# Reordering the first batch of an attention and gated-FFN kernel: scores ahead of the ninth turn, a shared last copy, one strided sum, three idle matmuls

## The chip, the core and the metric

The kernel runs on one core of a Trainium2 chip. The metric is the device time in microseconds (us) of one execution. The kernel before takes 767.75 us, the median of 3 runs (767.1 to 768.05). The profile of a kernel is taken of one execution, and its span (first to last instruction) is about 1.8 us shorter than the device time.

The engines go by short names: PE is TensorE, which does the matmuls, and PEld its weight loads; ACT is ScalarE, DVE is VectorE, POOL is GpSimd. The granted clock is the share of its full clock that the profile shows PE was given, over the stretch named.

## The reference

Four batches of 12416 rows of 128 numbers go through an attention with 32 inducing points and then through a gated feed-forward network (width 1536) with a gated residual:

```python
def mab(q, kv):                                   # C = 128
    s = scale * (q @ kv.transpose(0, 2, 1))
    s = s - s.max(-1, keepdims=True)
    a = np.exp(s)
    a /= a.sum(-1, keepdims=True) + 1e-09
    return a @ kv
h = mab(I, x)                                     # I: 32 inducing points
x = mab(x, h)                                     # what goes on
# ...
gelu = 0.5 * g * (1.0 + erf(g * inv_sqrt2))       # g = x @ w_gate
ffn_out = gelu * val @ w_out                      # val = x @ w_val
res_gate = 1.0 / (1.0 + np.exp(-(x @ w_res)))
return (x + res_gate * ffn_out).astype(np.float32)
```

## The kernel before

The first attention of a batch must read all of x before any row of the second one can begin. For batches 2 to 4 this is hidden behind the feed-forward work of the batch before. For the first batch nothing can hide it, and it is that stretch, some 32 us at the start, that the change edits.

x comes in 13 tiles: 12 of 8 blocks (128 rows each) and a last one of a single block. For each tile, DVE casts it to fp16 (`convert_hi`), PE turns it (transposes into PSUM, `turn_pe`) and ACT or DVE copies the result back. PE then takes the scores against the inducing points, ACT their exponentials, POOL adds these up (`step_e`, L168 and L171), and PE forms the weighted sums (`step_s`, L186).

```python
def turn_pe(b, k, eng=act):
    # ...
    for j in range(w):
        pe.transpose(tps[:, j, :], hi_t[b, k][:, j, :], identF)
    if eng is act:
        act.activation(xt[:, :w, :], tps[:, :w, :], AC.Copy, bias=0.0, scale=1.0)
    else:
        eng.tensor_copy(xt[:, :w, :], tps[:, :w, :])
```

The denominator of that softmax takes two strided sums on DVE, one over what POOL has added up, one over the exponentials of tile 11, which POOL does not add:

```python
def total(zb):
    # folded(e): a DVE sum of 128x256 to 128x32
    s = folded(e_of.pop("s"))
    yield pe.matmul(zb, ones, s, start=True, stop=False)
    # ... the exponentials of the tile of index 11
    s = folded(e_t["a", n0 // WIDE * WIDE][:, n0 % WIDE * M:(n0 % WIDE + w) * M])
    pe.matmul(zb, ones, e_t["a", nblk // WIDE * WIDE][:, :M], start=False, stop=False)
    yield pe.matmul(zb, ones, s, start=False, stop=True)
```

The order of the first batch, and what follows it:

```python
for n in range(ntile - 1):
    convert_hi(0, n + 1, ve)
    turn_pe(0, n, act if n < 10 and n % 2 == 0 else ve)
    # ... n == 0: the inducing points are turned, idle(2)
    if n == ntile - 2:
        turn_pe(0, n + 1, act)
    if n >= 1:
        step_e(n - 1)
    # ... n == 1: idle(2)
    if n >= 2:
        step_s(n - 2)
weight_cast(0, act)
step_e(ntile - 2)
step_e(ntile - 1)
weight_cast(1, act)
weight_cast(2, act)
step_s(ntile - 3)
zb = bank_g()[:, :M]
parts_of = total(zb)
next(parts_of)
step_s(ntile - 2)
step_s(ntile - 1)
next(parts_of)
idle(6, bank_g(), P)
weight_cast(3, act)
weight_cast(4, po)
turn_first_h(0, zb)          # reciprocal of zb, then ht = the attention's result, turned
exps("b", 0, 0, half, bank_g())   # the second attention's exponentials, from ht
# ... more of these, and the first layer of the feed-forward network from ht
```

After that the main loop obeys plans, strings in which G is a gate (matmuls, then a Gelu on ACT), P, Q and V are a product with its gates (the product u is DVE's), a number is so many output matmuls, and "i" is `idle(3)`: three matmuls of 512 columns on unused data, whose only purpose is to keep PE busy so that its granted clock does not fall. The first plan begins `"!GGGiPG VG 5GQ 5Q GQG6 P7G"`; "!" is `rest_of_first()`, the third part of the first layer.

The softmax here doesn't subtract the row's maximum and nothing guards it: scores larger than these inputs give would overflow.

Of the kernel before, what the change touches and what calls it, by code (L numbers as in the profile page):

```python
# [9 lines left out]
FP32 = mybir.dt.float32  # L10
# [3 lines left out]
AC = mybir.ActivationFunctionType  # L14
AL = mybir.AluOpType
# [3 lines left out]
def kernel(  # L19
# [23 lines left out]
    M = inducing.shape[0]  # L43
    F = moe_w_gate.shape[1]
    P = 128
# [4 lines left out]
    nblk = N // P  # L50
    PRE = 8
    ntile = (nblk + PRE - 1) // PRE
    Q = 4
    scale = 1.0 / math.sqrt(C)
    AX = mybir.AxisListType.X
# [25 lines left out]
    def bank_g():  # L81
        return ps_g.tile([P, TOK], FP32, name="g", tag="g")
# [54 lines left out]
    def turn_pe(b, k, eng=act):  # L137
        _, w = blocks_of(k)
        xt = sized(p_xt, w, P, "xt")
        xt_t[b, k] = xt  # L140
        tps = bank_g().bitcast(FP16).rearrange("p (k c) -> p k c", c=P)
        for j in range(w):
            pe.transpose(tps[:, j, :], hi_t[b, k][:, j, :], identF)
        if eng is act:
            act.activation(xt[:, :w, :], tps[:, :w, :], AC.Copy, bias=0.0, scale=1.0)
        else:
            eng.tensor_copy(xt[:, :w, :], tps[:, :w, :])


    nacc_t, acc_t, hra_t, hgv_t, ht_t, hf_t, hgt_t = {}, {}, {}, {}, {}, {}, {}  # L150
# [61 lines left out]

    def total(zb):

        def folded(e):
            s = p_sm.tile([P, WIDE], FP32, name="z", tag="z", bufs=5)
            ve.reduce_sum(s, e.rearrange("p (j m) -> p m j", m=M), axis=AX)
            return s

        s = folded(e_of.pop("s"))  # L220
        yield pe.matmul(zb, ones, s, start=True, stop=False)
        n0, w = blocks_of(ntile - 2)
        s = folded(e_t["a", n0 // WIDE * WIDE][:, n0 % WIDE * M:(n0 % WIDE + w) * M])
        pe.matmul(zb, ones, e_t["a", nblk // WIDE * WIDE][:, :M], start=False, stop=False)
        yield pe.matmul(zb, ones, s, start=False, stop=True)

    def idle(n, bank=None, w=TOK):

        bank = bank_f() if bank is None else bank
        for i in range(n):  # L230
            pe.matmul(bank[:, :w], warm[:, :P], warm[:, :w], start=True, stop=True)

    def finish_h(b, hs=None):
        if hs is None:
            hs = bank_g()
            pe.matmul(hs[:, 0:P + 1], strips.rearrange("p q m -> p (q m)"), nacc_t.pop(b),
                      start=True, stop=True)
        rz = p_h.tile([P, 1], FP32, name="rz1", tag="rz1")
        if b == 0:
            ve.tensor_copy(rz, hs[:, P:P + 1])  # L240
        else:
            ve.reciprocal(rz, hs[:, P:P + 1])
        hf = p_h.tile([P, P + 1], FP32, name="nacc", tag="nacc", bufs=1)[:, :P]
        ve.tensor_scalar(hf, hs[:, 0:P], rz, None, op0=AL.mult)
        hf_t[b] = hf

        hra = p_h.tile([P, 2, P], FP16, name="hra", tag="hra")
        hra_t[b] = hra
        po.memset(hra[2 * M:, 0, :], 0.0)
        po.memset(hra[:2 * M, 1, :], 0.0)  # L250
        po.tensor_copy(hra[2 * M:, 1, :], hf[2 * M:, :])
        po.tensor_tensor(hra[3 * M:, 1, :], hf[3 * M:, :], hra[3 * M:, 1, :], AL.subtract)

        if b not in hgv_t:
            hgv_t[b] = p_h.tile([P, F], BF16, name="hgv", tag="hgv")

    def turn_first_h(b, zb):

        na = nacc_t[b]
        tp = bank_g()[:, :P]  # L260
        pe.matmul(tp, na[:, 0:P], strips.rearrange("p q m -> p (q m)"), start=True, stop=True)
        idle(6, None, P)
        zi = e_of["zi"] = p_h.tile([P, M], FP32, name="zi", tag="zi", bufs=1)
        ve.reciprocal(zi, zb)
        ht = p_h.tile([P, P], FP16, name="ht", tag="ht")
        ve.tensor_tensor(ht.rearrange("p (q m) -> p q m", m=M),
                         tp.rearrange("p (q m) -> p q m", m=M),
                         zi.unsqueeze(1).to_broadcast([P, Q, M]), AL.mult)
        ht_t[b] = ht
        hgv_t[b] = p_h.tile([P, F], BF16, name="hgv", tag="hgv")  # L270
# [12 lines left out]
    def first_layer_out(b, c, bank):  # L283
        ve.tensor_scalar(hgv_t[b][:, c:c + TOK], bank, parts, None, op0=AL.mult)
# [54 lines left out]
    def ones_b(b, j0, j1):  # L339
        t0 = j0 // WIDE * WIDE  # L340
        z = e_of["z", b, t0][:, j0 - t0:j1 - t0]
        ve.reciprocal(z, z)

    def weights_b(b, k, j0=0, j1=None, eng=po, by_pe=False):

        n0, w = blocks_of(k)
        j1 = w if j1 is None else j1
        n = j1 - j0
        if j0 == 0:
            rt_t[b, k] = sized(p_rt, w, P, "rt")  # L350
        t0 = (n0 + j0) // WIDE * WIDE
        o = n0 + j0 - t0
        z = e_of["z", b, t0]
        ev = e_of["t", b, t0].rearrange("p (j m) -> p j m", m=M)
        a2 = p_sm.tile([P, PRE, Q, M], FP16, name="a2", tag="a2")
        eng.tensor_tensor(  # L356
            a2[:, :n],
            ev[:, o:o + n, :].unsqueeze(2).to_broadcast([P, n, Q, M]),
            z[:, o:o + n].unsqueeze(2).unsqueeze(3).to_broadcast([P, n, Q, M]), AL.mult)
        rt = rt_t[b, k][:, j0:j1, :]  # L360
        if by_pe:
            def turned():
                tps = bank_f().bitcast(FP16).rearrange("p (k c) -> p k c", c=P)
                for j in range(n):
                    pe.transpose(tps[:, j, :], a2[:, j].rearrange("p q m -> p (q m)"), identF)
                ve.tensor_copy(rt, tps[:, :n, :])
            return turned
        else:
            sy.dma_start_transpose(rt, a2[:, :n].rearrange("p j q m -> p (j q m)"))
# [160 lines left out]
    pieces = []  # L530
# [17 lines left out]
    def weight_cast(i, eng):  # L548
        dst, src, w = pieces[i]
        if eng is act:  # L550
            act.activation(dst, staged.pop(i)[:, :w], AC.Copy, bias=0.0, scale=1.0)
        else:
            eng.tensor_copy(dst, staged.pop(i)[:, :w])
# [5 lines left out]
    def step_e(n):  # L559
        n0, w = blocks_of(n)  # L560
        exps("a", 0, n0, n0 + w, bank_v())
        if n < ntile - 2:
            add_up(n0, w)

    def step_s(n):
        n0, w = blocks_of(n)
        accumulate(0, n0, n0 + w, n == 0, n == ntile - 1)
# [2 lines left out]
    hi_t[0, 0] = p_hl.tile([P, PRE, P], FP16, name="hi", tag="hi")  # L570
    ve.tensor_copy(hi_t[0, 0][:, :half], xf_t[0, 0][:, :half])
    act.activation(hi_t[0, 0][:, half:], xf_t[0, 0][:, half:], AC.Copy, bias=0.0, scale=1.0)
    for n in range(ntile - 1):
        convert_hi(0, n + 1, ve)
        turn_pe(0, n, act if n < 10 and n % 2 == 0 else ve)
        if n == 0:
            i1t_ps = bank_g()
            pe.transpose(i1t_ps[:, :M], ind_f, ident[:M, :M])
            ve.tensor_copy(I1T, i1t_ps[:, :M])
            idle(2)  # L580
        if n == ntile - 2:
            turn_pe(0, n + 1, act)
        if n >= 1:
            step_e(n - 1)
        if n == 1:
            idle(2)
        if n >= 2:
            step_s(n - 2)
    weight_cast(0, act)
    step_e(ntile - 2)  # L590
    step_e(ntile - 1)
    weight_cast(1, act)
    weight_cast(2, act)
    step_s(ntile - 3)
    zb = bank_g()[:, :M]
    parts_of = total(zb)
    next(parts_of)
    step_s(ntile - 2)
    step_s(ntile - 1)
    next(parts_of)  # L600
    idle(6, bank_g(), P)
    weight_cast(3, act)
    weight_cast(4, po)
    turn_first_h(0, zb)
    exps("b", 0, 0, half, bank_g())
# [14 lines left out]
            turned()  # L620
    first_layer(0, TOK, layers[:, TOK:])
    first_layer_out(0, TOK, layers[:, TOK:])
    weight_cast(5, po)
    ones_b(0, half, WIDE)
    weights_b(0, 0, half, PRE)
    for i in range(6, len(pieces)):
        weight_cast(i, po)
    later = [(t0, min(t0 + WIDE, nblk)) for t0 in range(WIDE, nblk, WIDE)]

    gel = konst.tile([P, 1], FP32, name="gel")  # L630
# [2 lines left out]
    def rest_of_first():  # L633
        layers = bank_v()
        first_layer(0, 2 * TOK, layers[:, :TOK])
        rs, hs = layers[:, TOK:TOK + P], layers[:, TOK + P:TOK + 2 * P + 1]
        pe.matmul(rs[:64, :], ht_t[0][:, :64], wR, start=True, stop=True)
        pe.matmul(hs[:, :P], strips.rearrange("p q m -> p (q m)"), nacc_t.pop(0)[:, :P],
                  start=True, stop=True)
        zi = e_of.pop("zi")  # L640
        for q in range(Q):
            pe.matmul(hs[q * M:(q + 1) * M, P:P + 1], zi, ident[:, 0:1], start=True, stop=True)
        first_layer_out(0, 2 * TOK, layers[:, :TOK])
        finish_h(0, hs)
        res_layer(0, ve, rs)

    plan_first = [
        "!GGGiPG VG 5GQ 5Q GQG6 P7G",
        "Q6 GQA 10RP 8A1GQR 3P 7Q",
        "G7Q G7P 7GP6 P4R7 P VGG8G *",  # L650
        "P9 P5A8 P2 4P 12PG 12GVG",
# [245 lines left out]
```

## Time and profile before

| | before |
|---|---|
| device time, median of 3 | 767.75 us |
| span of the profiled execution | 765.3 us |
| its mean granted clock of TensorE | 0.997 |
| first Gelu of the main loop (ACT) | 32.46 us |
| end of the 19th Gelu | 42.89 us |

This is the line of busy shares of the profile page (busy us, share of the span, number of instructions):

```profile
PE 743.0 (97%) x9623; PEld 432.5 (57%) x9623; DVE 737.1 (96%) x739; ACT 744.5 (97%) x1496; POOL 469.2 (61%) x463
```

Three engines are full, so only the stretches where one of them must wait can be shortened. The prediction below reads where they are. The next lines are ACT's timeline in the kernel before, at the start of the main loop; the columns are start, length, engine, line, operation, output<-input, and in brackets the idle time ahead and what ended it.

```profile
32.46 6.66 ACT L432 ACTIVATE ge<-g 128x512 f32<-128x512 f32 x13
39.50 1.08 ACT L432 ACTIVATE ge<-g 128x512 f32<-128x512 f32 x2 [0.38 <-PE g L421]
40.83 2.06 ACT L432 ACTIVATE ge<-g 128x512 f32<-128x512 f32 x4 [0.24 <-PE g L421]
```

ACT runs 13 Gelus without a pause, then waits twice for a slow PE, 0.38 and 0.24 us. The 19 Gelus, all that ACT runs ahead of its first tanh, take 42.89 - 32.46 = 10.43 us.

### The profile page before, as it was taken

The page shows a single profiled execution, that of the slowest core. Times are in us where ns is not written, and L with a number is a line of the kernel's source. Part 1 is how long each engine was busy: PE and PEld are TensorE (multiplying, and loading weights), DVE is VectorE, ACT ScalarE, POOL GpSimd, SP SyncE. Part 2 cuts the span into 40 slices and gives each one's busy share as a digit, 9 for nine tenths or more (in the row PEclk, how much of TensorE's full clock was granted, in tenths as well). Part 3 has the DMA queues.
Part 4 walks back from the last instruction along what each step waited for, and adds up shares of the span by engine and source line. Part 5 has one row for each costly group of instructions (what it writes and reads, how often), then busy time and mean ns, then how long its engine had stood idle before and what let it go on. Part 6 is the DMA issues. An engine that isn't in the chain of part 4 may idle for free.

```text
span 765.3 us, 23989 instructions
## 1 busy us (share of the span) xinstructions
PE 743.0 (97%) x9623; PEld 432.5 (57%) x9623; DVE 737.1 (96%) x739; ACT 744.5 (97%) x1496; POOL 469.2 (61%) x463
## 2 busy tenths in 40 slices
PE   9999999999999999999999999999999999999997
PEld 6555565566555555565655555565565555555554
DVE  5799999999999999989999999999999999999997
ACT  5799999999999999999999999999999999999997
POOL 3646998612786989623486789752277664543444
PEclk9999999999999999999999999999999999999999
DMA  9325597500165578601044567730105431101111
GB/s 360 110 57 144 138 240 159 130 30 30 50 123 117 115 178 208 156 32 43 16 105 87 129 167 194 173 108 30 43 29 118 88 85 43 43 29 43 44 43 46
DMA packets 118449, 78.16 MB, mean 102 GB/s; under 512 B 96672, under 2 KB 99392, under 8 KB 118336
## 3 DMA queue, kind: packets, MB, share of 16 engines
q1 hardware_dynamic: 118288, 76.60, 38.4%
q8 instruction: 75, 1.23, 0.6%
q14 instruction: 38, 0.31, 0.1%
q10 hardware_dynamic: 48, 0.02, 0.0%
HBM read 27.87 MB, written 25.43 MB: 70 GB/s over the span
## 4 chain that ended last, share of the span: by engine, by line
PE 47%; ACT 33%; issue 10%; DVE 6%; DMA 1%; POOL 1%; SPq 0%; DVEq 0%; ACTq 0%; POOLq 0%
ACT ge L432 24%; PE f L455 21%; PE g L421 12%; PE v L421 7%; DVE u L426 5%; PE g L463 3%; ACT th L469 3%; ACT at L474 3%; DMA xf<-in_x_dram 1%; ACT fe L483 1%; ACT e L171 1%; PE g L168 1%; DVE th L487 1%; POOL lo L127 1%; ACT L171 1%
## 5 line engine op out<-in xcount | busy, mean ns | idle before, releaser
L426 DVE TENSOR_TENSOR u<-ge,v 128x1024 bf16<-128x1024 f32 x584 | 670.8, 1211 | 5.1 <-PE v L421 1.3
L432 ACT ACTIVATE ge<-g 128x512 f32<-128x512 f32 x1164 | 605.3, 659 | 1.8 <-PE g L421 1.6
L455 PEld LDWEIGHTS <-u 128*128 128x128 bf16 x4656 | 269.8, 98 | 214.3 <-issue 209.7
L455 PE MATMUL f<-wO,u 128*128 128x128 bf16 x4656 | 373.6, 220 | 4.1 <-DVE th L487 0.8
L421 PE MATMUL g<-rt,hgv 32*128 32x512 f16 x1152 | 335.7, 379 | 7.3
L421 PE MATMUL v<-rt,hgv 32*128 32x512 f16 x1152 | 221.5, 385 | 1.8 <-DVE u L426 1.4
L488 POOL TENSOR_TENSOR at<-at,th 128x512 f32<-128x512 f32 (+1 forms) x99 | 123.7, 1250 | 130.0 <-ACT ge L432 37.6
L421 PEld LDWEIGHTS <-hgv 32*128 32x128 bf16 x2400 | 73.7, 91 | 85.8 <-issue 20.0
L484 POOL TENSOR_TENSOR th<-th,fe 128x512 f32<-128x512 f32 (+1 forms) x33 | 39.7, 1202 | 97.1 <-ACT fe L483 97.1
L356 POOL TENSOR_TENSOR a<-e,z 128x1024 f16<-128x1024 f32 (+1 forms) x48 | 89.8, 1881 | 6.8 <-DMA rt<-a 3.6
L127 POOL TENSOR_TENSOR lo<-xf,hi 128x1024 f16<-128x1024 f32 x36 | 76.9, 2137 | 0.2
L463 PE MATMUL g<-hra,rt 128*128 128x128 f16 x768 | 71.4, 219 | 1.5
L474 ACT ACTIVATE at<-g 128x512 f32<-128x512 f32 (+1 forms) x100 | 63.9, 649 | 0.2
L469 ACT ACTIVATE th<-g 128x512 f32<-128x512 f32 (+1 forms) x100 | 63.5, 647 | 0.3 <-PE g L421 0.2
L463 PEld LDWEIGHTS <-rt 128*128 128x128 f16 x768 | 50.6, 97 | 10.2 <-issue 8.0
L487 DVE SCALAR_TENSOR_TENSOR th<-th,f 128x512 f32<-128x512 f32 (+1 forms) x67 | 45.4, 678 | 3.2 <-PE f L455 1.7
L121 POOL CAST hi<-xf 128x1024 f16<-128x1024 f32 x36 | 37.4, 1039 | 14.4 <-DMA xf<-in_x_dram 10.4
L485 POOL TENSOR_TENSOR at<-at,fe 128x512 f32<-128x512 f32 (+1 forms) x33 | 39.7, 1203 | 0.0
L332 POOL TENSOR_TENSOR a<-e 128x512 f32<-128x512 f32 (+1 forms) x12 | 15.5, 1289 | 22.2 <-ACT e L171 22.2
L168 PEld LDWEIGHTS <-xt 128*128 128x128 f16 x768 | 23.3, 96 | 3.1 <-issue 2.5
L171 ACT ACTIVATE e<-g 128x512 f32<-128x512 f32 (+3 forms) x40 | 20.9, 602 | 1.9 <-PE g L168 1.8
L335 POOL TENSOR_TENSOR a<-a 128x256 f32<-128x256 f32 (+8 forms) x48 | 20.0, 417 | 3.8
(138 smaller groups left out, 262.3 us busy)
## 6 DMA issues: line engine op xcount, KB each, us to landing
out_dram<-at SPq DMA_DIRECT2D x96, 256.0 KB, 2.1
xf<-in_x_dram SPq DMA_DIRECT2D x39, 512.0 KB, 4.2
ge<-in_x_dram SPq DMA_DIRECT2D x9, 512.0 KB, 7.0
rt<-a SPq DMA_TRANSPOSE x48, 3.1
xt<-hi SPq DMA_TRANSPOSE x36, 3.6
ge<-in_moe_w_gate_dram SPq DMA_DIRECT2D x1, 512.0 KB, 8.9
ge<-in_moe_w_val_dram SPq DMA_DIRECT2D x1, 512.0 KB, 7.6
ge<-in_moe_w_out_dram SPq DMA_DIRECT2D x1, 512.0 KB, 6.8
```

What stands on the lines that cost most here:

```text
L127: eng.tensor_tensor(lo[:, :w, :P], xf_t.pop((b, k))[:, :w, :], hi_t[b, k][:, :w, :], AL.subtract)
L356: eng.tensor_tensor(a2[:, :n], ev[:, o:o + n, :].unsqueeze(2).to_broadcast([P, n, Q, M]), z[:, o:o + n].unsqueeze(2).unsqueeze(3).to_broad ...
L421: pe.matmul(*t[n], start=True, stop=True)
L426: ve.tensor_tensor(u[:, :n], ge_t.pop(value)[:, :n], v_t.pop(value)[:, :n], AL.mult)
L432: act.activation(ge_t[i][:, h * TOK:h * TOK + n], gb[:, :n], AC.Gelu, bias=0.0, scale=1.0)
L455: pe.matmul(self.ffn[:, k, :], u_t[self.gi, si][:, o:o + P], wO[:, fc, :], start=first, stop=not self.todo, skip_group_check=True)
L463: pe.matmul(bank[:, k * P:(k + 1) * P], rt_t[self.b, self.k][:, self.j0 + k, :], hra_t[self.b][:, s, :], start=True, stop=True)
L469: act.activation(self.th[:, :self.tw], self.mix(0), AC.Tanh, bias=0.0, scale=0.5)
L474: act.activation(self.at[:, :self.tw], self.mix(1), AC.Copy, bias=0.0, scale=1.0)
L484: po.tensor_tensor(th, th, fe, AL.mult)
L487: ve.scalar_tensor_tensor(th, th, 1.0, f, AL.add, AL.mult)
L488: (ve if self.gi == ngrp - 1 else po).tensor_tensor(at, at, th, AL.add)
```

## The change

The change wants the first batch to end sooner and the clock to hold at the start of the main loop. The ninth turn, whose tile arrives late, moves behind scores and sums that are ready. The last tile's cast goes to POOL and the last big copy is split between DVE and ACT. The two strided sums become one addition and one sum. ACT's four weight casts move behind the last exponentials of the first attention, so that these are not held up. DVE's third scaling of the first layer gets ahead of a reciprocal that waits for POOL. Three idle matmuls are added behind the second product ("VGi"), and seven small ones are taken out. Two changes are easy to miss in the diff: without the condition `n < 10` the copy of tile 10 goes from DVE to ACT, and the copy of the small last tile goes from ACT to DVE.

```diff
--- before.py
+++ after.py
@@ -141,10 +141,11 @@
         tps = bank_g().bitcast(FP16).rearrange("p (k c) -> p k c", c=P)
         for j in range(w):
             pe.transpose(tps[:, j, :], hi_t[b, k][:, j, :], identF)
-        if eng is act:
-            act.activation(xt[:, :w, :], tps[:, :w, :], AC.Copy, bias=0.0, scale=1.0)
-        else:
-            eng.tensor_copy(xt[:, :w, :], tps[:, :w, :])
+        h = w // 2 if eng is None else w * (eng is not act)
+        if h > 0:
+            ve.tensor_copy(xt[:, :h, :], tps[:, :h, :])
+        if h < w:
+            act.activation(xt[:, h:w, :], tps[:, h:w, :], AC.Copy, bias=0.0, scale=1.0)
 
 
     nacc_t, acc_t, hra_t, hgv_t, ht_t, hf_t, hgt_t = {}, {}, {}, {}, {}, {}, {}
@@ -212,17 +213,15 @@
 
     def total(zb):
 
-        def folded(e):
-            s = p_sm.tile([P, WIDE], FP32, name="z", tag="z", bufs=5)
-            ve.reduce_sum(s, e.rearrange("p (j m) -> p m j", m=M), axis=AX)
-            return s
-
-        s = folded(e_of.pop("s"))
-        yield pe.matmul(zb, ones, s, start=True, stop=False)
+        s = e_of.pop("s")
         n0, w = blocks_of(ntile - 2)
-        s = folded(e_t["a", n0 // WIDE * WIDE][:, n0 % WIDE * M:(n0 % WIDE + w) * M])
-        pe.matmul(zb, ones, e_t["a", nblk // WIDE * WIDE][:, :M], start=False, stop=False)
-        yield pe.matmul(zb, ones, s, start=False, stop=True)
+        e = e_t["a", n0 // WIDE * WIDE][:, n0 % WIDE * M:(n0 % WIDE + w) * M]
+        ve.tensor_tensor(s[:, :w * M], s[:, :w * M], e, AL.add)
+        z = p_sm.tile([P, WIDE], FP32, name="z", tag="z", bufs=5)[:, :M]
+        ve.reduce_sum(z, s.rearrange("p (j m) -> p m j", m=M), axis=AX)
+        yield
+        pe.matmul(zb, ones, e_t["a", nblk // WIDE * WIDE][:, :M], start=True, stop=False)
+        yield pe.matmul(zb, ones, z, start=False, stop=True)
 
     def idle(n, bank=None, w=TOK):
 
@@ -259,7 +258,7 @@
         na = nacc_t[b]
         tp = bank_g()[:, :P]
         pe.matmul(tp, na[:, 0:P], strips.rearrange("p q m -> p (q m)"), start=True, stop=True)
-        idle(6, None, P)
+        idle(5, None, P)
         zi = e_of["zi"] = p_h.tile([P, M], FP32, name="zi", tag="zi", bufs=1)
         ve.reciprocal(zi, zb)
         ht = p_h.tile([P, P], FP16, name="ht", tag="ht")
@@ -570,36 +569,41 @@
     hi_t[0, 0] = p_hl.tile([P, PRE, P], FP16, name="hi", tag="hi")
     ve.tensor_copy(hi_t[0, 0][:, :half], xf_t[0, 0][:, :half])
     act.activation(hi_t[0, 0][:, half:], xf_t[0, 0][:, half:], AC.Copy, bias=0.0, scale=1.0)
-    for n in range(ntile - 1):
+    for n in range(ntile - 2):
+        if n == 8:
+            step_e(n - 1)
+            step_s(n - 2)
+        if n == 9:
+            step_s(n - 2)
         convert_hi(0, n + 1, ve)
-        turn_pe(0, n, act if n < 10 and n % 2 == 0 else ve)
+        turn_pe(0, n, act if n % 2 == 0 else ve)
         if n == 0:
             i1t_ps = bank_g()
             pe.transpose(i1t_ps[:, :M], ind_f, ident[:M, :M])
             ve.tensor_copy(I1T, i1t_ps[:, :M])
             idle(2)
-        if n == ntile - 2:
-            turn_pe(0, n + 1, act)
-        if n >= 1:
+        if n >= 1 and n != 8:
             step_e(n - 1)
         if n == 1:
             idle(2)
-        if n >= 2:
+        if n >= 2 and n not in (8, 9):
             step_s(n - 2)
-    weight_cast(0, act)
+    convert_hi(0, ntile - 1, po)
+    turn_pe(0, ntile - 2, None)
+    turn_pe(0, ntile - 1, ve)
+    step_e(ntile - 3)
+    step_s(ntile - 4)
+    step_e(ntile - 1)
     step_e(ntile - 2)
-    step_e(ntile - 1)
-    weight_cast(1, act)
-    weight_cast(2, act)
     step_s(ntile - 3)
+    step_s(ntile - 2)
+    for i in (0, 1, 2, 3):
+        weight_cast(i, act)
     zb = bank_g()[:, :M]
-    parts_of = total(zb)
-    next(parts_of)
-    step_s(ntile - 2)
+    denominator = total(zb)
+    next(denominator)
     step_s(ntile - 1)
-    next(parts_of)
-    idle(6, bank_g(), P)
-    weight_cast(3, act)
+    next(denominator)
     weight_cast(4, po)
     turn_first_h(0, zb)
     exps("b", 0, 0, half, bank_g())
@@ -620,11 +624,6 @@
             turned()
     first_layer(0, TOK, layers[:, TOK:])
     first_layer_out(0, TOK, layers[:, TOK:])
-    weight_cast(5, po)
-    ones_b(0, half, WIDE)
-    weights_b(0, 0, half, PRE)
-    for i in range(6, len(pieces)):
-        weight_cast(i, po)
     later = [(t0, min(t0 + WIDE, nblk)) for t0 in range(WIDE, nblk, WIDE)]
 
     gel = konst.tile([P, 1], FP32, name="gel")
@@ -641,11 +640,16 @@
         for q in range(Q):
             pe.matmul(hs[q * M:(q + 1) * M, P:P + 1], zi, ident[:, 0:1], start=True, stop=True)
         first_layer_out(0, 2 * TOK, layers[:, :TOK])
+        weight_cast(5, po)
+        ones_b(0, half, WIDE)
+        weights_b(0, 0, half, PRE)
+        for i in range(6, len(pieces)):
+            weight_cast(i, po)
         finish_h(0, hs)
         res_layer(0, ve, rs)
 
     plan_first = [
-        "!GGGiPG VG 5GQ 5Q GQG6 P7G",
+        "!GGGiPG VGi 5GQ 5Q GQG6 P7G",
         "Q6 GQA 10RP 8A1GQR 3P 7Q",
         "G7Q G7P 7GP6 P4R7 P VGG8G *",
         "P9 P5A8 P2 4P 12PG 12GVG",
```

Lines of the changed kernel are numbered a little differently: the Gelu of L432 is L431, the scores of L168 are L169, the sums of L186 are L187.

## The prediction

> **What bounds the kernel now.** I read the table of busy shares first: PE 97%, DVE 96%, ACT 97% of a span of 765.3 us. Three engines are full, so no single one gives much. Then I cut the span into three stretches by the table of windows: the first batch (to 32.46 us, where ACT starts its first Gelu), the run-in of the main loop (32.46 to 46), and the rest.
>
> ```profile
> core 0: us, PE busy (x) PEld busy (x) DVE busy (x) ACT busy (x) POOL busy (x), PEclk, DMA share, GB/s
> 33.73:37.14 3.41, 2.76 (x23) 0.95 (x22) 3.38 (x4) 3.41 (x8) 3.10 (x7) 1.00 0.19 38
> 37.14:40.57 3.43, 3.21 (x25) 1.54 (x24) 3.43 (x4) 3.01 (x6) 0.62 (x1) 0.51 0.42 81
> ...
> 32.46:46.00 13.54, 12.32 (x112) 5.72 (x111) 12.98 (x16) 12.88 (x27) 5.47 (x9) 0.87 0.16 31
> 46.00:745.00 699.00, 685.66 (x8766) 395.42 (x8762) 688.70 (x665) 697.54 (x1407) 440.86 (x424) 1.00 0.39 97
> ```
>
> The last line says what the change can be worth. From 46 to 745 us ACT is busy 697.54 of 699.00 us: it has 1.46 us of holes. All the edits lie before about 36 us, and the order of ACT's work after that is unchanged. So the end moves by two things only: how much earlier ACT starts its first Gelu (32.46 now), and how much of ACT's idle 0.66 us (13.54 - 12.88) in the run-in goes away. The second line shows where that idle time is from: for 3.43 us PE ran at a granted clock of 0.51.
>
> Next the chain of waits, in order of time, through the first batch:
>
> ```profile
> 4.79 11.07 DMA xf<-in_x_dram
> ...
> 15.88 0.75 DVE hi L121
> ...
> 16.68 0.62 PE g L143 x8
> 17.30 0.34 PE v L168 x8
> 17.64 0.57 PE f L186 x16
> 18.21 0.55 PE g L143 x8
> ...
> 22.22 0.74 POOL a L211
> ...
> 22.98 0.61 DVE z L217
> ...
> 24.85 0.29 DVE nacc L198
> 25.14 0.51 DVE z L217
> ...
> 26.76 0.30 DVE ht L266
> ```
>
> The ninth tile of x (tile 8) lands at 15.86; until then the DMA queues are the bound and no reordering helps. From 16.68 PE is nearly gapless (turns L143, scores L168, sums L186, one set per tile each 1.32 us) to the end of the last sums at 24.8. Then comes the flaw that the change aims at: the second strided sum (L217, the tile of index 11) starts only at 25.14, although its exponentials were ready at 23.13, because on DVE it is queued behind the copy of the accumulator. The reciprocal, and with it ht at 26.76, follow that sum. The first exponentials of the second half follow ht at 27.46. The last look is at the timeline of ACT and DVE around them:
>
> ```profile
> 24.57 1.05 ACT L551 ACTIVATE wV<-ge 128x1024 bf16<-128x1024 f32 x1
> 27.46 0.73 ACT L171 ACTIVATE e<-g 128x128 f32<-128x128 f32 x2 [1.83 <-PE g L168]
> ...
> 32.18 0.65 DVE L284 TENSOR_SCALAR hgv<-v,parts 128x512 bf16<-128x512 f32 x1
> ```
>
> ACT has 1.83 us of slack before the second exponentials.
>
> **What the Trainium skill says.** (1) "TensorE: Matmul & The Clock Gate", Part 1: the clock is either half or full, decided over free-running windows of 3413 ns. The trace agrees: the slow spell is 3.43 us at about 0.5, and the 3.41 us before it is the window that failed. Where the windows fall is a matter of phase, so one run need not repeat another's. (2) The same page, Part 4: transposes do not count as PE activity in the same way. No run shows this yet; it matters if PE now waits between transposes. (3) "PSUM — Partial Sum Buffer", section on bank collisions: two reading engines must be kept apart on one bank too. That bears on the shared copy: its halves read one bank, and the built kernel has ACT's half wait for DVE, so they run one after the other. (4) "VectorE: DVE Perf Modes", the tier table: a reduction has only the plain mode. Here a 128x256 reduction takes 0.60 us.
>
> **The change part by part.** I walk the new queue of each engine with durations of the trace. From instruction start to the next engine's start: a turn 0.65, scores 0.39. PE per turn 0.46, scores 0.28, sums 0.57. ACT: a big copy 1.02, exponentials 0.38. DVE: a cast or copy 0.68. POOL: an add 0.73.
>
> Ninth turn. The scores of tile 7 wait for a DVE copy that is queued behind the cast of tile 8, so it ends at 17.22 in both kernels. Before, PE used the wait for the turn of tile 8 (16.68 to 17.25). Now that turn comes after scores 7 and sums 6, at 18.14. Nothing is saved: PE idles 0.6 us more, ACT's copy of tile 8 starts at 18.79 in place of 17.33, and scores 8 begins at 19.87 in place of 18.6. Turn 10 moves to 20.15, its ACT copy lasts until 21.84, and the exponentials of tile 9 to 22.12 behind it (20.70 before).
>
> Small last tile. Its cast moves from DVE (0.22 us, at 20.80) to POOL, queued behind the add of tile 9: 22.26 + 0.73 = 22.98, then about 0.27 (wR's cast of the same shape took 0.29 there). Its turn stands ahead of scores 10 in PE's queue, so PE, done with turn 11 at about 21.92, waits to about 23.30. This is 1.4 us of new waiting.
>
> Last big copy shared: half on DVE (about 0.36), then half on ACT (0.6). It is ready at about 23.1, before it can be used.
>
> Tail. Scores 10 to 23.64, sums 9 to 24.21, scores 12 and 11 to 24.53, their exponentials to 25.05 (23.13 before). Sums 10, 11, 12 on PE to 25.77. POOL's last add ends at 25.03, DVE's new add (128x256, about 0.38, scaled from 1.21 for 128x1024) at 25.45, the one reduction at 26.02. The denominator's matmul starts at 26.10 (25.70 before), the reciprocal at 26.54 (26.15), ht at 26.93 (26.76: there the six idle matmuls had delayed it). The one reduction in place of two takes back about 0.5 us and the idle ones 0.2, of the nearly 1 us that PE lost. Net: ht 0.17 us later.
>
> Weight casts. All four are now behind the last exponentials: 0.52 + 0.52 + 0.94 + 0.94 = 2.92 us by their spacing in the trace, from 25.0 to 27.9. The second exponentials, ready at 27.6, start at 27.9 (27.46). ACT then has 0.6 us less slack, but the 1024-wide exponentials wait for PE in any case (28.95 before, 29.12 now). So the first Gelu starts about 0.17 us later.
>
> Scaling ahead of the reciprocal. The third scaling of the first layer (32.18) now runs at about 31.6, as it no longer waits for POOL's sums. That is worth 0.56 on DVE, of which 0.44 goes to POOL's later start: the first product u begins at about 33.7 in place of 33.82, a gain of 0.1 us that DVE, not ACT, gets.
>
> Three more idle matmuls behind the second product: 3 x 0.21 = 0.64 us of PE, in the window that failed its test, mostly where PE waited for DVE. If the clock holds, ACT's 0.62 us of waits for PE (0.38 at 39.1, 0.24 at 40.6) mostly go: 0.45 us net.
>
> Sum: +0.17 for the start and -0.45 if the clock holds, say two in three: about -0.15 expected. As my walk may overstate the wait for POOL's cast (the exact queue of that moment decides), I shade it to -0.45: 767.75 - 0.45 = 767.3.
>
> **Rivals.** *The tail gets its full gain.* If the small cast does not hold PE, PE ends its sums near 24.5, and ht comes at about 25.9; ACT's casts then end near 26.8 and the second exponentials start 0.6 to 0.9 us earlier; with the clock held the time is about 766.4. For it: the old tail's 2.0 us between ready exponentials and their sum is real. Against it: POOL's queue order, add 9 and then the cast. *A cold spell moves to the first batch.* New PE gaps of 0.8 and 1.4 us and fewer idle matmuls could make a window at 20 to 27 us fail; at half clock one set of turn, scores and sums takes up to twice its 1.32 us, and as about one such set in a window lies on the path, it costs some 1 us: 768.5 to 769 (an estimate). Against it: the old kernel kept 1.00 there with 0.7 us of gaps. *ACT's casts become the bound*, if the exponentials end still later than 25.05: each 0.1 us later is 0.1 us lost, 768.2.
>
> **Range and chances.** All of it moves within about 1.2 us either way, and the three runs before already span 0.95 us. Predicted 767.3, range 766.3 to 768.5. Two per cent would be 15 us, twenty times any term: within 2% is near certain.
>
> **What would show it.** The copy of tile 8 on ACT near 18.8. A wait of PE for POOL's cast at 22 to 23.3 (if absent, my main loss falls). ACT casts ending within 0.3 us of the second exponentials. First Gelu at 32.6. Granted clock 1.00 from 37 to 41, and no ACT wait for PE at 39 to 41. I am wrong if the first Gelu moves by more than 0.6 us either way, or if ACT gains or loses time after 46 us.

## The result

The changed kernel takes 766.93 us, the median of 4 runs (766.53 to 767.04); before in the same rounds takes 767.78 (767.1 to 768.05, 4 runs). The ratio is 0.9989, with a 95% interval of 0.9972 to 1.0007. Ratios here are the mean time of one kernel's runs over that of the other's of the same rounds, so they are not quite the ratio of the medians. The difference of the medians is -0.85 us, which these four runs alone do not tell from zero.

The stretches of the changed kernel, in the columns of the table of windows in the prediction (stretch, us, busy us of PE, PEld, DVE, ACT, POOL with counts, granted clock, DMA share, GB/s):

```profile
0.00:32.46 32.46, 28.98 (x535) 20.17 (x536) 18.88 (x42) 20.26 (x34) 13.73 (x26) 1.00 0.71 273
32.46:46.00 13.54, 12.50 (x116) 5.75 (x115) 12.59 (x17) 12.88 (x28) 5.55 (x9) 1.00 0.16 31
46.00:745.00 699.00, 685.92 (x8767) 395.63 (x8766) 688.95 (x665) 697.70 (x1407) 440.56 (x424) 1.00 0.39 97
```

The clock is 1.00 in the run-in (0.87 before). Yet ACT is busy for the same 12.88 us of it as before, and from 46 us on nothing changed that could matter (697.70 against 697.54). Both facts need an explanation, and the first batch comes first. Its chain of waits, in order of time (start, length, engine, output, line):

```profile
20.75 1.02 ACT xt L148
...
22.19 0.72 POOL a L212
22.91 0.24 POOL his L121
23.20 0.23 PE g L143
24.52 1.32 PE f L187 x34
...
27.07 0.30 DVE ht L265
```

The walk of the prediction is here step for step: POOL's add of tile 9, then its small cast (`his`), then PE's turn of it at 23.20 (predicted 23.30), the last sums, and ht at 27.07 (26.93; before 26.76). ACT's timeline in the changed kernel:

```profile
18.81 1.02 ACT L148 ACTIVATE xt<-g 128x1024 f16<-128x1024 f16 x1 [0.74 <-PE g L143]
22.68 0.60 ACT L148 ACTIVATE xt<-g 128x512 f16<-128x512 f16 x1 [0.63 <-DVE xt L146]
...
27.77 0.72 ACT L172 ACTIVATE e<-g 128x128 f32<-128x128 f32 x2
32.77 3.51 ACT L431 ACTIVATE ge<-g 128x512 f32<-128x512 f32 x7
36.93 6.03 ACT L431 ACTIVATE ge<-g 128x512 f32<-128x512 f32 x12 [0.65 <-PE g L420]
```

The copy of tile 8 starts at 18.81 (predicted 18.79). The second half of the shared copy waits 0.63 us for DVE's half, so the halves run one after the other. The second exponentials start at 27.77, with no wait behind the weight casts. The first Gelu comes at 32.77, 0.31 us later than before.

The last line holds the surprise. The two waits of before, 0.62 us together, are gone, and one of 0.65 us stands in their place, at 36.28. PE's timeline shows why:

```profile
34.86 0.37 PE L420 MATMUL g<-rt,hgv 32*128 32x512 f16 x1
35.17 0.82 PE L230 MATMUL f<-lo 128*128 128x512 f16 x3
36.14 0.44 PE L454 MATMUL f<-wO,u 128*128 128x128 bf16 x5
```

The new idle matmuls (L230) stand behind a gate and ahead of five output matmuls and the next gate. In before the output matmuls began at 35.10; now they begin at 36.14, and the gate that ACT waits for is behind them.

In these two profiled executions the 19th Gelu ends at 42.89 before and at 42.96 after, and the executions themselves took 767.10 and 767.01: they are equal. So where do the medians' 0.85 us come from? The executions of before that the experiments ran beside their kernels, 20 in all, show it. Here they are by their mean granted clock:

| mean clock | executions of before | mean time, us |
|---|---|---|
| 0.999 | 3 | 766.38 |
| 0.997 | 4 | 767.08 |
| 0.994 and 0.995 | 8 | 767.79 |
| 0.992 | 5 | 768.60 |

In the profiled execution of before (0.997) one window of 3.43 us ran at 0.51, which lowers a mean over 765.3 us by 3.43 x 0.49 / 765.3 = 0.0022. So the rows stand, by this estimate, for none, one, two and three slow windows, and each costs about (768.60 - 766.38) / 3 = 0.74 us. The profile before showed one of the milder executions. The sorting is rough: a mean clock also takes in the end of the run, and one profiled execution with one slow window (e3 below) has 0.998. The four executions of the changed kernel all had 0.999 or 1.000.

### The profile page after: what moved, and what is told of

It is laid out like the page before. It is cut to its first block, busy times and chain, and to the rows that moved or that the text cites. A ratio compares the mean times of both kernels' runs of the same rounds, so it can differ in the third digit from the quotient of the medians.

```text
span 765.2 us, 23976 instructions
## 1 busy us (share of the span) xinstructions
PE 742.3 (97%) x9617; PEld 431.6 (56%) x9617; DVE 736.2 (96%) x738; ACT 745.6 (97%) x1497; POOL 468.7 (61%) x464
## 4 chain that ended last, share of the span: by engine, by line
PE 47%; ACT 34%; issue 9%; DVE 5%; POOL 2%; DMA 1%; SPq 0%; DVEq 0%; ACTq 0%; POOLq 0%
ACT ge L431 25%; PE f L454 21%; PE g L420 12%; PE v L420 7%; DVE u L425 4%; PE g L462 3%; ACT th L468 3%; ACT at L473 3%; DMA xf<-in_x_dram 1%; ACT fe L482 1%; PE g L169 1%; ACT e L172 1%; DVE th L486 1%; POOL lo L127 1%; ACT L172 1%
## 5 line engine op out<-in xcount | busy, mean ns | idle before, releaser
L431 ACT ACTIVATE ge<-g 128x512 f32<-128x512 f32 x1164 | 605.5, 660 | 1.8 <-PE g L420 1.6
L169 PEld LDWEIGHTS <-xt 128*128 128x128 f16 x768 | 23.2, 96 | 4.5 <-issue 2.7
L482 ACT ACTIVATE fe<-f 128x512 f32<-128x512 f32 (+1 forms) x33 | 21.0, 637 | 0.0
```

Of the source, the lines that this page charges most:

```text
L431: act.activation(ge_t[i][:, h * TOK:h * TOK + n], gb[:, :n], AC.Gelu, bias=0.0, scale=1.0)
```

## The experiments

The theory to be tested had three parts. The clock: the three idle matmuls are what makes the changed kernel faster, all else together loses a little. The front: the ninth turn and the small cast on POOL cost the 0.31 us of the first Gelu and hide a gain of the tail. The placement: the idle matmuls behind the gate cost 0.65 us that they need not. The rivals were that the reordering of the first batch gives the gain, that the small cast alone is the cause of the front's loss, and that ACT would wait about as long wherever the idle matmuls stand.

Three groups of kernels ran, each group beside its own runs of before, with medians of 767.49 (9 executions), 767.56 (10, which include those of the first group) and 768.22 (10). All gave correct results. Where kernels of different groups are compared below (the changed kernel with any other, e1 with e11, e8 with e9 and e10), it is by their medians and their traces, and not by a ratio of the same rounds. Every experiment's row also gives the end of the 19th Gelu in its profiled execution, for a reason that the table shows.

| kernel | median us (lowest to highest, executions) | ratio to before, 95% interval | first Gelu | end of 19th | profiled execution |
|---|---|---|---|---|---|
| before | 767.78 (767.1-768.05, 4) | 1 | 32.46 | 42.89 | 767.10 |
| after | 766.93 (766.53-767.04, 4) | 0.9989, 0.9972-1.0007 | 32.77 | 42.96 | 767.01 |
| e1_idle_alone | 766.82 (766.65-767.88, 5) | 0.9997, 0.9983-1.0011 | 32.50 | 42.68 | 766.82 |
| e2_no_idle | 768.15 (767.69-768.58, 5) | 1.001, 0.9998-1.0023 | 32.64 | 44.01 | 768.43 |
| e3_small_cast_dve | 766.65 (766.36-767.69, 5) | 0.9992, 0.998-1.0005 | 32.57 | 43.85 | 767.69 |
| e4_ninth_undone | 766.2 (766.07-767.29, 6) | 0.9987, 0.9975-1.0 | 32.16 | 42.35 | 766.08 |
| e5_both_undone | 765.65 (765.46-766.67, 5) | 0.998, 0.9967-0.9992 | 31.57 | 41.75 | 765.55 |
| e6_idle_ahead | 766.44 (766.28-766.62, 5) | 0.9987, 0.9974-1.0001 | 32.99 | 42.82 | 766.62 |
| e7_whole_copy | 765.93 (765.38-766.31, 4) | 0.9981, 0.9967-0.9994 | 31.40 | 41.58 | 765.38 |
| e8_best | 764.67 (764.46-766.32, 5) | 0.9969, 0.9957-0.9982 | 30.99 | 40.82 | 764.67 |
| e9_two_sums | 765.9 (765.71-766.52, 6) | 0.9977, 0.9964-0.999 | 32.13 | 41.96 | 765.82 |
| e10_scaling_behind | 764.99 (764.61-766.34, 6) | 0.9966, 0.9953-0.9978 | 31.01 | 40.84 | 764.75 |
| e11_before_idle_ahead | 766.38 (766.25-767.25, 6) | 0.9984, 0.9971-0.9997 | 32.53 | 42.36 | 766.42 |

The profiled time less the end of the 19th Gelu is 723.7 to 724.4 us in every row. So what follows differs by 0.7 us at most, where the end of the 19th Gelu differs by 3.2 us (40.82 to 44.01): most of what sets these kernels apart is decided in the first 44 us, and two numbers of a profile are enough to compare them: when the first Gelu starts, and how long the first 19 take.

### e1_idle_alone: the idle matmuls alone, added to before

```diff
-        "!GGGiPG VG 5GQ 5Q GQG6 P7G",
+        "!GGGiPG VGi 5GQ 5Q GQG6 P7G",
```

> The kernel before with nothing but the three idle matmuls behind the second product. Theory A (the measured 0.85 us is the clock: the kernel before falls to half clock near 37 us in most executions, the idle matmuls prevent it): granted clock 1.00 from 30 to 46 us, time 0.6 to 1.2 us under the kernel before, so as fast as or faster than the changed kernel, because the first Gelu stays at 32.46 and is not 0.31 us later. Theory B (the gain is from the first batch's new order or from the scaling of the first layer going ahead): time within 0.3 us of the kernel before, as the idle matmuls only delay the first products by about 0.9 us, as in the trace of the changed kernel (36.14 against 35.10).

Measured: 766.82 us, 0.67 under before's median of this group. The means are nearer (ratio 0.9997, and its interval includes 1). The 19 Gelus took 10.18 us in the profiled execution at a clock of 1.00, with the same wait of ACT, 0.65 us. By the medians this one letter gives nearly as much as the whole change, which is in the range of theory A, that the gain is the clock's. By the ratio of the means it would be theory B's "within 0.3 us". One execution of the five, the slowest (767.88), has a clock of 0.997. So this run leans to theory A and does not settle it; e2, which takes the letter out again, does.

### e2_no_idle: the changed kernel without the added idle matmuls

```diff
-        "!GGGiPG VGi 5GQ 5Q GQG6 P7G",
+        "!GGGiPG VG 5GQ 5Q GQG6 P7G",
```

> The changed kernel without the three idle matmuls. Theory A: the clock falls to a half for one window near 37 us in the trace, ACT waits for PE there, and the time is 0.3 to 0.5 us over the kernel before, the loss of the new order standing alone (first Gelu 0.31 us later). Theory B: about as the changed kernel, 0.5 to 1 us under the kernel before.

Measured: 768.15 us, 0.66 over before of its group; all five executions have a clock of 0.992 to 0.995. First the line of the table of windows of this kernel, then one of ACT's timeline:

```profile
34.93:45.05 10.12, 9.96 (x76) 5.37 (x75) 8.33 (x8) 8.18 (x17) 2.77 (x4) 0.50 0.21 42
```

```profile
40.27 1.08 ACT L431 ACTIVATE ge<-g 128x512 f32<-128x512 f32 x2 [0.53 <-PE g L420]
```

The clock is half for 10.12 us, three windows of 3.4 where I had expected one, and ACT is busy 8.18 us of them. The 19 Gelus take 11.37 us, 1.18 more than the 10.19 in the changed kernel. The four executions of the changed kernel had a clock of 0.999 or 1.000, so in these runs the three idle matmuls are what holds it. Without them the change gains nothing: by the median it is a small loss, which its interval (0.9998 to 1.0023) does not tell from zero. This also shows the spell at its full length, which the profiled execution of before did not.

### e3_small_cast_dve: the last tile's cast back on DVE

```diff
-    convert_hi(0, ntile - 1, po)
+    convert_hi(0, ntile - 1, ve)
```

> The changed kernel with the cast of the small last tile back on VectorE. If PE's wait of 1.0 us for that cast at 22.2 to 23.2 us is what delays the tail (my step): the turn of the small tile follows turn 11 directly, at about 22.0, scores 10 at 22.1, the first Gelu about 0.9 us earlier than in the changed kernel (near 31.9), time 0.7 to 1.0 us under the changed kernel. Rival: scores 10 wait for ACT's copy of tile 10 (to 21.8) and the exponentials behind the shared copy, and the gain at the first Gelu is under 0.4 us.

Measured: 766.65 us, 0.28 under the changed kernel, with the first Gelu at 32.57, 0.20 earlier. The profiled execution happened to be this kernel's slowest; the first batch can still be read from it, as its slow window comes later:

```profile
35.00:38.42 3.42, 3.27 (x21) 1.29 (x21) 1.50 (x2) 1.67 (x5) 2.63 (x4) 0.50 0.19 38
```

So the idle matmuls did not hold the clock here. They start at 34.96, as the slow window begins, run at half clock, and ACT waits 1.75 us for the eighth gate in place of 0.65. They make a slow window rare and do not rule it out: of the 57 executions of the kernels that have them, 7 have a clock of 0.996 or 0.997, besides this one; of before's 20, 17 have 0.997 or less. PE's timeline of the first batch:

```profile
21.96 0.22 PE L143 MATMUL g<-identF,his 128*128 128x128 f16 x1
...
23.36 0.64 PE L187 MATMUL f<-xf,e 128*32 128x128 f32 x13 [0.65 <-issue]
```

The turn of the small tile now runs at 21.96 instead of 23.20, as intended. But PE pauses 0.65 us inside the sums of tile 9, between the third and the fourth matmul, with no releaser in the trace ("issue"), and most of the win is gone. So undoing the cast alone does not win the front back: my expectation fell, and the rival's size, a gain of less than 0.4 us, was right, though not for the rival's reason. The pause sits at a fixed place. In the thirteen profiles, the pauses of PE of over 0.1 us without a releaser between 8 and 33 us come after the same number of its records (matmuls and weight loads): after 450 (0.10 to 0.41 us) or after 706, which is this one (0.65 here, 0.21 in e1). The two are 256 records apart, and the place does not move with the program. What the pause is stays open.

### e4_ninth_undone: the ninth turn in its old place, the cast still on POOL

```diff
-        if n == 8:
-            step_e(n - 1)
-            step_s(n - 2)
-        if n == 9:
-            step_s(n - 2)
         convert_hi(0, n + 1, ve)
# ...
-        if n >= 1 and n != 8:
+        if n >= 1:
             step_e(n - 1)
# ...
-        if n >= 2 and n not in (8, 9):
+        if n >= 2:
             step_s(n - 2)
```

> The changed kernel with only the ninth turn back ahead of the scores and sums; the small cast stays on GpSimd. Theory N (the ninth turn's order is the whole loss in the first batch; GpSimd's cast is then early enough): first Gelu within 0.2 us of the run with both undone (31.57), time near 765.7. Theory C (GpSimd's queue also costs once the rest is fast: add 9, then the cast, then add 10): PE waits for the cast again, for some 0.5 us near 21.4 to 22.5, first Gelu near 32.0 to 32.3, time near 766.3.

Measured: 766.2 us, 0.73 under the changed kernel, the first Gelu at 32.16, 0.61 earlier. PE's timeline:

```profile
22.59 0.23 PE L143 MATMUL g<-identF,his 128*128 128x128 f16 x1 [1.17 <-POOL his L121]
```

PE still waits 1.17 us for POOL's cast, only 0.6 us earlier. So the moved ninth turn costs 0.6 us by itself. Theory C, that POOL's queue costs too once the rest is faster, held: the first Gelu and the time are where it put them, though the wait is 1.17 us and not 0.5. Theory N, that the ninth turn is the whole loss, fell.

### e5_both_undone: both of these undone

```diff
# e4's edit, and
-    convert_hi(0, ntile - 1, po)
+    convert_hi(0, ntile - 1, ve)
```

> The changed kernel with the small cast back on VectorE and the ninth turn back ahead of the scores and sums. If the reordering at the ninth turn only makes PE idle 0.6 us longer (my step): a further 0.4 to 0.6 us earlier than with the cast alone, first Gelu near 31.4, time 1.2 to 1.6 us under the changed kernel. Rival: the ninth turn's order is hidden behind the DMA landings of tiles 9 and 10 or behind ACT's copies, and this run equals the one with the cast alone within 0.2 us.

Measured: 765.65 us, 1.28 under the changed kernel; the first Gelu at 31.57, 1.20 earlier. PE's timeline:

```profile
22.95 0.35 PE L169 MATMUL v<-I1T,xt 128*128 128x32 f16 x8 [0.32 <-ACT e L172]
```

The scores of tile 11 run at 22.95 with only 0.32 us of waiting ahead. The time is in the expected range. In the profiles the two gains do not add: 0.20 and 0.61 alone, 1.20 together. With the ninth turn back, the cast is worth 0.59 (e4 to e5); with the cast back, the ninth turn is worth 1.00 (e3 to e5), of which up to 0.65 is the pause of e3, nearly absent here (the sixteen matmuls take 0.80 us). So the two faults cost about 0.6 us each, and they are what kept the better tail from showing.

### e6_idle_ahead: the changed kernel with its idle matmuls ahead of the gate

```diff
-        "!GGGiPG VGi 5GQ 5Q GQG6 P7G",
+        "!GGGiPG ViG 5GQ 5Q GQG6 P7G",
```

> The changed kernel with its three idle matmuls ahead of the gate matmul of that step in place of behind it. Theory P (behind it they stand in the way of the first products, and ACT's wait of 0.65 us for the eighth gate at 36.3 comes from them; ahead of it PE has time to spare): clock still 1.00 to 46 us, ACT's wait there under 0.2 us, time 0.4 to 0.65 us under the changed kernel, near 766.4. Rival: the eighth gate waits for something else (GpSimd's cast of the output weights, a bank), ACT's wait stays, time as the changed kernel; or the clock falls in some executions and the time spreads to 767.5.

Measured: 766.44 us, 0.49 under the changed kernel. PE's timeline:

```profile
34.92 0.82 PE L230 MATMUL f<-lo 128*128 128x512 f16 x3
35.67 0.38 PE L420 MATMUL g<-rt,hgv 32*128 32x512 f16 x1
35.99 0.45 PE L454 MATMUL f<-wO,u 128*128 128x128 bf16 x5
```

The same three matmuls run at nearly the same time. But now it is the seventh gate that stands behind them (35.67), which ACT reaches only at 36.0, and the eighth runs at 36.37 instead of 36.51 although the first Gelu is 0.22 us later. PE's pauses ahead of the seventh gate (0.09 us) and ahead of the output matmuls (0.15, from 35.99 to 36.14) in the changed kernel are gone. ACT's wait of 0.65 us is gone too; its single records show pauses of 0.09 and 0.10 us in its place. The 19 Gelus take 9.83 us (10.19 behind the gate), at a clock of at least 0.998 in all executions. Theory P, that the place makes the wait, held: the clock does not need that place. Of the 0.65 us, 0.36 came back in the profile.

### e7_whole_copy: e5 with the last big copy whole on DVE

```diff
-    turn_pe(0, ntile - 2, None)
+    turn_pe(0, ntile - 2, ve)
```

> The run with both undone, with the last big copy whole on VectorE, not shared. Theory S (sharing is a loss: ACT's half waits for VectorE's half as both read one PSUM bank, and the exponentials of tile 10 queue behind it): exponentials of tile 10 about 0.5 us earlier (near 22.0), scores of tile 11 near 22.5, first Gelu 0.2 to 0.45 us earlier than 31.57, time near 765.3. Rival: the tail is set by PE's sums, and the first Gelu does not move by over 0.1 us.

Measured: 765.93 us (765.38 to 766.31) against e5's 765.65 (765.46 to 766.67). The two overlap, so the time does not settle it. In the profiled executions e7 is the earlier one, 31.40 against 31.57. These 0.17 us are less than theory S asked for (0.2 to 0.45), more than the rival's 0.1, and within what the front varies by itself (see e8), so neither is shown. No gain of sharing the copy is seen: its halves read one bank one after the other (ACT waits 0.48 us for DVE's half in e5), and ACT's part lies ahead of ACT's exponentials of tile 10, which start at 22.52 in e5 and at 21.83 here.

### e8_best: e7 with the idle matmuls ahead of the gate

```diff
-        "!GGGiPG VGi 5GQ 5Q GQG6 P7G",
+        "!GGGiPG ViG 5GQ 5Q GQG6 P7G",
```

> Both undone, whole copy on VectorE, and the idle matmuls ahead of the gate matmul. If the gains add: 0.4 to 0.65 us under the run with the whole copy, 764.7 to 765.0, some 2.6 us under the kernel before. Rival: the earlier ramp is bound by VectorE's chain ahead of the first product u, or the clock falls, and the time is not under 765.3.

Measured: 764.67 us, 2.9 under before and 2.3 under the changed kernel, and faster than before beyond doubt (interval 0.9957 to 0.9982). Its run-in, in the table of windows:

```profile
30.99:46.00 15.01, 14.13 (x134) 6.67 (x132) 14.40 (x18) 14.81 (x31) 7.39 (x10) 1.00 0.16 35
```

The first Gelu is at 30.99 and ACT is then busy for 14.81 of 15.01 us. The 19 Gelus take 9.83 us, as in e6: the gains of front and placement add in the profile. The time is 1.26 us under e7's, more than the 0.4 to 0.65 expected; the placement gives 0.35 of that (10.18 to 9.83). The front is 0.41 us earlier than e7's although its program is the same, through a shorter pause of PE in the sums of tile 9 (0.81 us for the sixteen matmuls, 1.10 in e7) and about 0.1 us of an earlier landing of tile 8. So single profiles of the front differ by 0.2 to 0.4 us for no reason of the program. One execution of e8 took 766.32 at a clock of 1.000; its cause is open.

### e9_two_sums: e8 with before's denominator

```diff
# total() as in before: two strided sums, the first of which has its matmul
# ahead of the sums of the last, small tile
```

> The best kernel so far (764.67) with the old denominator: two strided sums on VectorE, the second behind the copy of the accumulator, in place of an add and one sum. If the single sum is a part of the change that pays (my step: the second sum in VectorE's queue is what held the reciprocal): the reciprocal and the first Gelu come 0.4 to 0.6 us later, time 765.1 to 765.3. Rival: the matmuls of the last sums set the reciprocal in any case, or ACT's weight casts do; the first Gelu moves by under 0.2 us, time under 764.9.

Measured: 765.9 us, 1.2 over e8 of the group before and 0.9 over e10 of its own; the first Gelu at 32.13, 1.14 later. DVE's timeline, first of e8, then of this kernel:

```profile
23.72 0.60 DVE L221 TENSOR_REDUCE z<-a 128x32 f32<-128x256 f32 x1
24.82 0.36 DVE L263 RECIPROCAL zi<-g 128x32 f32<-128x32 f32 x1 [0.30 <-PE g L224]
```

```profile
24.66 0.29 DVE L199 COPY nacc<-f 128x128 f32<-128x128 f32 x1 [0.84 <-PE f L187]
24.87 0.58 DVE L218 TENSOR_REDUCE z<-e 128x32 f32<-128x256 f32 x1
25.96 0.36 DVE L265 RECIPROCAL zi<-g 128x32 f32<-128x32 f32 x1 [0.50 <-PE g L226]
```

With two sums the second runs behind the copy of the accumulator, at 24.87, and the reciprocal comes at 25.96 instead of 24.82. The copy itself is 0.42 us later too (24.66 against 24.24 in e8), since the first sum's matmul stands in PE's queue ahead of the last tile's sums. The one sum is thus worth 1.1 us in the profile and 0.9 to 1.2 by the medians, about twice what I had put it at.

### e10_scaling_behind: e8 with the third scaling back behind POOL's sums

```diff
# weight_cast(5, po), ones_b, weights_b and the weight casts behind them
# stand ahead of rest_of_first() again, as in before
```

> The best kernel so far with the third scaling of the first layer back behind GpSimd's sums of the second exponentials. VectorE's first product u comes about 0.3 us later (from 32.09 to 32.4). Theory: ACT is the bound from its first Gelu on, which does not move, so the time changes by under 0.2 us. Rival: the first products on PE and with them the eighth gate wait for u, ACT waits at about 35 us for some 0.3 us, and the time is 0.2 to 0.4 us over 764.67.

Measured: 764.99 us (764.61 to 766.34), against 764.67 for e8 in another group: within the spread. In the profile the reciprocal waits 0.46 us for POOL again and the first product u starts at 32.36 instead of 32.09, but the first Gelu (31.01) and the 19 Gelus (9.83 us) are as in e8. DVE's gain does not reach ACT, which sets the end. The time alone does not resolve it: the medians differ by 0.32 us, which is in the rival's range, but the rival's wait of ACT at 35 us is not in the trace.

### e11_before_idle_ahead: before with the idle matmuls, ahead of the gate

```diff
-        "!GGGiPG VG 5GQ 5Q GQG6 P7G",
+        "!GGGiPG ViG 5GQ 5Q GQG6 P7G",
```

> The kernel before with nothing but the three idle matmuls ahead of that gate matmul. If the clock is worth what the executions of the kernel before show (766.15 at a mean clock of 0.999, 767.1 at 0.997, 767.65 at 0.994): clock at 0.998 or more in all executions, ACT without a wait of over 0.2 us at 36 us, time 765.9 to 766.3, some 1.4 us under the kernel before and 0.5 us under the run with the idle matmuls behind the gate. Rival: the clock still falls in some executions, or the time stays near 766.8.

Measured: 766.38 us, just above the expected range, and 0.44 under e1's. One letter in one string does more than the whole change. The clock did fall in one execution of the six (767.25, at 0.997), so the rival was right in that. The number is also that of before's own executions at a clock of 0.999 (766.38), which is what a kernel with no slow window and no new wait should take.

## Why the prediction was right or wrong

The class and the range were right: 766.93 lies in 766.3 to 768.5. But the range is 2.2 us wide, and that the number came near (-0.45 predicted, -0.85 measured) is luck in part. The expected -0.15 was shaded to -0.45 because the walk might overstate the wait for POOL's cast. That wait was shorter (1.02 us for 1.4) but ended where the walk had it, and the first Gelu came later than predicted; a term of the clock about three times as large (1.3 us for 0.45) made up for it. The walk through the first batch was right in its order and near in its times: tile 8's copy at 18.81 (18.79), the scores behind it at 19.89 (19.87), PE held by POOL's cast until 23.20 (23.30), the reciprocal at 26.61 (26.54), the casts' end at 27.77 (27.9). One line was read a little wrong: the second sum of before starts at 25.06 in the timeline, and 25.14 is where its part of the chain begins. The clock in the run-in was 1.00, as hoped.

**"ACT's 0.62 us of waits for PE mostly go: 0.45 us net" failed.** The waits went, and one of 0.65 us came in their place, because the idle matmuls stand between a gate and the work ahead of the next gate. e6 moves them across the gate and gets 9.83 us for the 19 Gelus instead of 10.19. I counted 0.64 us of PE as filling idle time and did not ask which ACT instruction was next behind it. In the sum, this step gave 10.43 - 10.19 = 0.24 us in the profiles instead of 0.45.

**The cold spell was sized from one mild execution.** The profile before showed one slow window; before has two or three of them in 13 of 20 executions. From the table by clock, the mean is (0 x 3 + 1 x 4 + 2 x 8 + 3 x 5) / 20 = 1.75 windows, at 0.74 us each 1.3 us, and that, not 0.62 us, is what was there to be saved. The sum then closes: before without slow windows 766.38, plus 0.31 for the later front, plus 0.44 for the placement (e1 less e11) is 767.13, against 766.93 measured and 767.78 before. So the change loses 0.75 us in two places and wins about 1.3 in one. The skill's clock-gate page (Part 1, cited above) has the window right, as e2's 10.12 us show. The spells begin at 37.14 us in before, 34.93 in e2 and 35.00 in e3, 2.2 us apart, which is no multiple of 3.4, so the windows lie differently from execution to execution; that this decides how many of them an execution gets fits the scatter, but no run shows it. Why a window fails stays open as well: in e2 PE was busy for 9.96 of the 10.12 slow us by the profile, and the clock stayed at half.

**Front, +0.17 predicted, +0.31 in the profile:** right in direction, 0.14 too small, within what the front varies by itself (e7 and e8).

**Single sum, mis-sized:** I put it at 0.5 us; e9 shows 1.1. I did not count that the first sum's matmul also holds the last tile's sums on PE.

**The rival "the tail gets its full gain if the small cast does not hold PE" fell** as it was stated: e3 took the cast's wait away and won 0.20 us. Both faults had to go: the ninth turn cost 0.6 and both together 1.2 us (e4, e5). With both undone, e5 at 765.65 is better than the 766.4 that the rival named.

**The rival of a cold spell moving to the first batch** did not happen: the clock is 1.00 up to 32.46 us in the changed kernel with its longer waits of PE. Whether transposes count for the gate (the skill's Part 4, cited above) no run tells.

**"ACT's casts become the bound"** did not come true, but only just. They end at 27.77, exactly where the second exponentials start. Yet the exponentials start 0.36 us after PE begins their scores (27.41), and before, where ACT had idled for 1.83 us, it was 0.36 us as well (27.10 to 27.46); in e8 it is 25.63 to 25.99. So the casts held nothing up, and a shorter chain ahead of the exponentials would be held by them.

**Scaling, "a gain of 0.1 us that DVE, not ACT, gets":** half right. In the changed kernel u starts at 33.87, no earlier than before (33.82), as the later front eats it; e10 shows 0.27 us for DVE and nothing for ACT.

What stays open: the pause of PE inside a group of sums (0.65 us in e3); the single executions that are about 1 us or more above the rest of their kernel where the mean clock does not account for them (those of e1, e4, e5 and e11 have 0.997, that of e3 had a slow window, but e8's has 1.000); and whether the shared copy costs anything (e5 against e7). Three parts of the change were never undone alone: ACT's casts behind the exponentials, the copy of tile 10 on ACT, and the seven small idle matmuls taken out. The clock and the placement do not hang on them, as e1 and e11 show on before itself.

## What to carry to other kernels

Before sizing a loss of clock from a profile, look at the mean clock of all executions: the profiled one may be among the mild, and what a spell costs on average is what preventing it is worth. Idle matmuls that hold the clock belong ahead of a result that the full engine will not reach yet, not ahead of one that it needs next; moved by one letter here they gave 0.4 to 0.5 us more. When a change bundles several moves, undo them singly and together, since two moves that each hide the same gain look harmless one at a time.

## What the Trainium skill lacked or had wrong

- "TensorE: Matmul & The Clock Gate", Part 1 and its summary: the advice is to leave no idle gap of about 3 us and more. In before the stretch ahead of the slow window had PE busy for 2.76 of 3.41 us by the profile, and the clock fell all the same; in e2 it stayed at half while PE was busy for 9.96 of 10.12 us. The page gives no share of busy time that a window needs, nor how matmuls with 32 rows count.
- The same page says that the number of cold matmuls varies from run to run and that the ramp is under 1% of a typical span. It lacks that a mid-kernel spell can last one to three windows in the same program (mean clock 0.999 to 0.992 in 20 executions of before; three windows seen in e2's trace), at about 0.74 us each here.
- No page that I found says where matmuls that only keep the clock up should stand: behind the gate they cost ACT a wait of 0.65 us (after, e1), ahead of it pauses of 0.09 and 0.10 us (e6, e11).
- No page that I found explains pauses of PE without a releaser inside a group of fp32 matmuls (0.65 us in e3; sixteen matmuls took 0.64, 0.80 and 1.10 us in different places and executions; those over 0.1 us come after 450 or 706 of PE's records, 256 apart, whatever the kernel). "Runtime: NRT & Kernel Launch", Instruction fetch mechanics, calls the cost of a fetch mostly hidden; whether these pauses are fetches no run here shows.
